# Window attention woven into a two-layer product: transposes and value products of a token tile issued one or two slots later, tiles at another spacing

## The chip, the cores and the metric

One core of a Trainium2 chip runs the whole program. The metric is the device time of one execution in microseconds (us). The kernel before takes 881.43 us, the median of three runs (880.12 to 882.33). Differences under 0.3% (2.6 us) are about what a measurement of this kernel cannot tell from none.

## The reference

All data is float32. 4 sequences of 576 tokens have 8 heads of 64 channels; a token sees itself and the 63 tokens before it. The result, as 2304 tokens of 512 channels, goes through two two-layer products.

```python
scores = scale * np.matmul(q, k.transpose(0, 1, 3, 2))
mask = (rel >= 0) & (rel < window)                  # window = 64
attn = np.exp(scores - max); attn = attn / (np.sum(attn, axis=-1, keepdims=True) + 1e-09)
x = np.matmul(attn, v)                              # -> (2304, 512)
h = x @ w_in;  g = np.maximum(0.01 * h, h);              y = g @ w_out      # 512 -> 2048 -> 512
h = y @ w_in2; g = np.maximum(h, 0) + np.log1p(np.exp(-np.abs(h))); out = g @ w_out2
```

## The kernel before

Each large product is made of three TensorE products of rounded halves (`three`, L530 to L533), because an operand is kept as a high and a low part (`xh`, `xl`, `gh`, `gl`).

The tokens are cut into 6 chunks of 384, a chunk into 3 tiles of 128 (`TPC`). For a chunk and one of 16 slices `j` of the hidden layer there is a step: `gemm1(c, j)` makes 12 products into the PSUM tile `ph` and has ScalarE and VectorE make `g`, `gh` and `gl` from it; `gemm2`, two steps behind (`SKEW`), makes 12 products into the four PSUM tiles `o`. The attention of chunks 0 and 1 is done in the head, whose order is written out by hand (`HEAD`) and which the change does not touch. The attention of chunks 2 to 5 (tiles 6 to 17) is woven into the steps of earlier chunks: a step has two slots, one ahead of `gemm1` and one ahead of `gemm2`, so an even slot's work stands before the 12 products of `gemm1` and an odd slot's before the 12 of `gemm2`. Chunk 2 is woven into a visit of 8 steps (16 slots), chunks 3, 4 and 5 each into a visit of 16 steps (32 slots). `attention_slots` says which piece of which tile goes into which slot; the slots of a tile are counted from `s`, the slot of its scores:

- `tile_a` (slot s-1): VectorE transposes of q and k (L690, L693), ScalarE's scaled copy `qbd`, and a copy on GpSimd.
- `tile_bp` (s): the scores, 32 small TensorE products into two PSUM tiles `ps` (L703). Then for each half of the heads `tile_bm` (mask, VectorE, L719), `att_bn` (maximum, VectorE) and `att_be` (four exponentials with their sums, ScalarE, L439).
- `att_bs`, `att_bx` (s and s+1): reciprocals of the sums on VectorE, and one multiplication on GpSimd for each half (L452), which gives `sm`.
- `att_cp`, `att_ca`: four TensorE transposes of `sm` for each half into PSUM tiles `pt` (L461), and their copies `at` on ScalarE (L467).
- `tile_d`: the value products `po` (32 on TensorE, L733: 16 with the rows `vs` of v, then 16 with `vn`), then `xh` on ScalarE (L743) and `xl` on VectorE (L744). The last tile's `xh` and `xl` complete the chunk, whose `gemm1` follows in the next visit.
- Loads on SyncE's queue: `load_qk(t + 1)` in slot s+1 (for even tiles the blocks of two tiles, in 32 or 64 transfers; nothing for odd ones), and `load_v(t + 1)` beside `tile_d`.

`ps`, `pt` and `po` share two PSUM buffers in this stretch (tag `att`), so a tile's scores need both, its transposes need both, and its value products need one. `sm` has three buffers in SBUF, `at` two, the rows of v three.

The kernel is written in a framework whose planner fixes each engine's order when the program is built: it goes by program order, passes over an instruction whose inputs or buffers it does not yet expect to be ready, and goes by its own estimates of time. At run time each engine works through its list in that order.

Of the kernel before, what the change touches and what calls it, by code (L numbers as in the profile page):

```python
# [20 lines left out]
def tile_window_attention_two_mlps(  # L21
# [40 lines left out]
    TPC = T // P  # L62
# [432 lines left out]
    def new_x(m, c):  # L495
        xh, xl = (x_tile(nm, f"{nm}_{m}_{c}", [P, NK, T], F32R) for nm in ("xh", "xl"))
        X[m, c] = (xh, xl)
        return xh, xl
# [247 lines left out]
    def attention_slots(c, n_slots):  # L746

        at = {n: [] for n in range(n_slots)}
        x = new_x(0, c)
        for n in range(TPC):  # L750
            t = c * TPC + n
            s = 1 + (n_slots - 8) * n // (TPC - 1)
            two = ((t, 0), (t, 1))
            at[s - 1].append((tile_a, (t,)))
            at[s].append((tile_bp, (t,)))
            at[s] += [(f, (g,)) for g in two for f in (tile_bm, att_bn)]
            at[s].append((att_be, (two[0],)))
            at[s + 1] += [(f, (two[0],)) for f in (att_bs, att_bx)]
            at[s + 1] += [(f, (two[1],)) for f in (att_be, att_bs, att_bx)]
            if t + 1 < NT // P and t + 1 != BY_DVE:  # L760
                at[s + 1].append((load_qk, (t + 1,)))
            at[s + 3] += [(f, (g,)) for f in (att_cp, att_ca) for g in two]
            at[s + 5].append((tile_d, (t, *x)))
            if t + 1 < NT // P:
                at[s + 5].append((load_v, (t + 1,)))
        return at

    def ticker(keys):
# [67 lines left out]
    for item in HEAD:  # L836
        n = len(item.rstrip("0123456789"))
# [39 lines left out]
    for n, (c, j, s, e, nxt) in enumerate(steps):  # L877
        if n < CUT + NF:
            continue
        if s:  # L880
            left = next(i for i in range(n, len(steps)) if steps[i][3]) - n + 1
            slots = attention_slots(nxt, 2 * left) if nxt is not None else {}
            slot = 0
        for u in range(2):
            for f, a in slots.get(slot, ()):
                f(*a)
            slot += 1
            if u == 0:
                gemm1(c, j)
        if c == NC - 1:  # L890
            for f, *a in prepare.get(j, ()):
                later(f, *a)
        if n >= SKEW:
            gemm2(*steps[n - SKEW][:4])
# [13 lines left out]
    for p in range(2, NF // 2):  # L908
        n = last_of[p - 2]
# [66 lines left out]
```

## Time and profile before

| | before |
|---|---|
| median of three runs | 881.43 us (880.12 to 882.33) |
| the profiled execution's own time | 884.99 us |
| its span, first to last instruction | 883.2 us |
| granted TensorE clock, mean of the span | 0.994 of full speed |
| TensorE matmul records busy | 854.2 us, 97% |
| VectorE, ScalarE, GpSimd busy | 538.1, 408.1, 49.5 us |

The profile is of one execution, which took 3.6 us more than the median of the runs. The stretch with which the change is concerned, the steps that carry attention, lies from about 152 to 440 us after the span's start. In the views, PE is TensorE, PEld its weight loads, DVE VectorE, ACT ScalarE, POOL GpSimd and SPq SyncE's queue of transfers. Matmuls overlap: a busy record covers one product from its start to its modelled end, and the next one starts before that.

### The profile page before, as it was taken

How to read it: one execution, taken by the hardware profiler on the slowest of the kernel's cores; microseconds unless marked ns; L12 is line 12 of the kernel's file. 1: busy time of each engine (PE TensorE's matmuls, PEld its weight loads, DVE VectorE, ACT ScalarE, POOL GpSimd, SP SyncE). 2: the span in 40 equal slices, each digit the busy share in tenths (PEclk: the TensorE clock that was granted, in tenths of full speed). 3: DMA queues.
4: the chain of work that ended last, by engine and by line, in shares of the span. 5: the costliest groups of instructions: out<-in, count | busy, mean ns of one | idle time of the engine just before them, and what ended most of it. 6: DMA issues, size and time to landing. Idle time of an engine off the chain costs nothing.

```text
span 883.2 us, 14592 instructions
## 1 busy us (share of the span) xinstructions
PE 854.2 (97%) x5424; PEld 799.9 (91%) x5424; DVE 538.1 (61%) x1052; ACT 408.1 (46%) x966; POOL 49.5 (6%) x66
## 2 busy tenths in 40 slices
PE   6799899999999999999999999999999999999998
PEld 5789899898999989999999999999999888888886
DVE  5798762535333233321357689777799986766664
ACT  6786652644434344442445532222244754545443
POOL 3111000211101011100000000000000000000000
PEclk9899999999999999999999999999999999999999
DMA  9767552243133420210132145544487544444432
GB/s 203 191 196 224 167 128 40 64 81 92 28 56 55 99 57 26 60 24 13 37 127 77 54 161 194 165 155 155 155 307 253 190 133 126 117 127 122 117 102 65
DMA packets 150278, 104.76 MB, mean 119 GB/s; under 512 B 104896, under 2 KB 129472, under 8 KB 150208
## 3 DMA queue, kind: packets, MB, share of 16 engines
q1 hardware_dynamic: 150208, 103.84, 41.3%
q8 instruction: 42, 0.69, 0.3%
q14 instruction: 28, 0.23, 0.1%
HBM read 75.50 MB, written 28.31 MB: 118 GB/s over the span
## 4 chain that ended last, share of the span: by engine, by line
PE 79%; DVE 6%; SPq 4%; DMA 4%; ACT 4%; issue 2%; POOL 1%; POOLq 0%; DVEq 0%; ACTq 0%
PE f L531 7%; PE f L532 7%; PE f L533 7%; PE ph L531 6%; PE ph L533 5%; PE ph L532 5%; PE o L531 5%; PE o L532 5%; PE o L533 5%; PE p_s L532 4%; PE p_s L531 4%; PE p_s L533 4%; SPq L336 3%; PE p_a L532 3%; PE p_a L531 3%; PE p_a L533 3%
## 5 line engine op out<-in xcount | busy, mean ns | idle before, releaser
L563 DVE TENSOR_TENSOR gl<-g,gh 128x384 fp32r<-128x384 f32 x96 | 58.2, 606 | 181.5 <-ACT gh L557 144.1
L531 PE MATMUL o<-gh,w 128*128 128x384 f32 x384 | 130.9, 341 | 2.4 <-ACT part L577 2.3
L531 PE MATMUL ph<-xh,w 128*128 128x384 f32 x384 | 131.4, 342 | 0.0
L532 PE MATMUL o<-gl,w 128*128 128x384 f32 x384 | 129.1, 336 | 0.3 <-DVE gl L563 0.2
L532 PE MATMUL ph<-xl,w 128*128 128x384 f32 x384 | 128.5, 335 | 0.0
L533 PE MATMUL ph<-xh,w 128*128 128x384 f32 x384 | 128.5, 335 | 0.0
L533 PE MATMUL o<-gh,w 128*128 128x384 f32 x360 | 121.0, 336 | 0.0
L551 ACT ACTIVATE g<-ph 128x384 f32<-128x384 f32 x96 | 46.9, 488 | 148.9 <-PE ph L533 148.7
L531 PE MATMUL f<-w,s 128*128 128x512 f32 x234 | 91.0, 389 | 0.0
L532 PE MATMUL f<-w,s 128*128 128x512 f32 x234 | 91.0, 389 | 0.0
L533 PE MATMUL f<-w,s 128*128 128x512 f32 x234 | 91.0, 389 | 0.0
L662 ACT ACTIVATE s<-s 128x512 f32<-128x512 f32 (+1 forms) x80 | 46.8, 588 | 72.8 <-DVE s L661 72.5
L531 PEld LDWEIGHTS o<-gh,w 128*128 128x128 f32 x384 | 72.6, 189 | 5.2 <-ACT part L577 2.5
L532 PEld LDWEIGHTS o<-gl,w 128*128 128x128 f32 x384 | 72.7, 189 | 0.8 <-DVE gl L563 0.8
L531 PEld LDWEIGHTS ph<-xh,w 128*128 128x128 f32 x384 | 72.1, 188 | 1.0
L664 DVE SCALAR_TENSOR_TENSOR s<-s,s 128x512 f32<-128x512 f32 (+1 forms) x80 | 50.7, 638 | 36.4 <-ACT s L662 36.0
L532 PEld LDWEIGHTS ph<-xl,w 128*128 128x128 f32 x384 | 72.2, 188 | 0.0
L533 PEld LDWEIGHTS ph<-xh,w 128*128 128x128 f32 x384 | 72.1, 188 | 0.0
L533 PEld LDWEIGHTS o<-gh,w 128*128 128x128 f32 x360 | 68.0, 189 | 0.0
L439 ACT ACTIVATE sm<-sm,nm 128x128 f32<-128x128 f32 x144 | 55.9, 390 | 24.5 <-DVE nm L428 24.4
L234 DVE TENSOR_TENSOR s<-s,s 128x512 fp32r<-128x512 f32 (+1 forms) x80 | 50.9, 638 | 12.8 <-ACT s L233 12.4
L233 ACT CAST s<-s 128x512 fp32r<-128x512 f32 (+1 forms) x80 | 46.0, 576 | 23.4 <-PE f L532 20.1
(169 smaller groups left out, 1645.5 us busy)
## 6 DMA issues: line engine op xcount, KB each, us to landing
wraw<-in_moe_w_out_dram SPq DMA_DIRECT2D x32, 512.0 KB, 4.7
wraw<-in_moe_w_in_dram SPq DMA_DIRECT2D x32, 512.0 KB, 4.7
s<-hd SPq DMA_DIRECT2D x64, 256.0 KB, 2.7
hd<-h_xh SPq DMA_DIRECT2D x12, 768.0 KB, 4.5
hd<-h_xl SPq DMA_DIRECT2D x12, 768.0 KB, 4.2
x2d<-x SPq DMA_DIRECT2D x24, 192.0 KB, 2.0
x_stage<-x2d SPq DMA_DIRECT2D x24, 192.0 KB, 2.5
out_dram<-s SPq DMA_DIRECT2D x18, 256.0 KB, 2.4
```

Of the source, the lines that this page charges most:

```text
L233: i = nc.scalar.copy(hi, a)
L234: j = nc.vector.tensor_tensor(lo, a, hi.bitcast(F32), ALU.subtract)
L336: nc.sync.dma_start(a[i * TB : (i + 1) * TB, p, off : off + n].rearrange("r (n c) -> r n c", c=TB), src[b, 2 * p + h, s : s + n, d : d + T ...
L439: nc.scalar.activation(sm[:, p, :], sm[:, p, :], AF.Exp, bias=nm[:, p : p + 1], accum_out=sums[:, p : p + 1],)
L531: nc.tensor.matmul(ps, wh, xh, start=start, stop=False)
L532: nc.tensor.matmul(ps, wh, xl, start=False, stop=False)
L533: nc.tensor.matmul(ps, wl, xh, start=False, stop=stop)
L551: nc.scalar.activation(g, ph, AF.Prelu, alpha=0.01)
L563: b = nc.vector.tensor_tensor(gl, g, gh.bitcast(F32), ALU.subtract)
L662: nc.scalar.activation(g, g, AF.Softplus)
L664: nc.vector.scalar_tensor_tensor(g, h, 0.0, g, ALU.max, ALU.add)
```

## The change

In the visits of 32 slots the scores of the three tiles stand in slots 1, 12 and 23 (before: 1, 13, 25), the transposes and their copies five slots after the scores (before: three), and the value products with the load of the next tile's v rows seven after (before: five). In the visit of 16 slots the scores stay in slots 1, 5 and 9, the transposes come four slots after them and the value products six. So there a tile's transposes come into the slot of the next tile's scores (slots 5 and 9), ahead of them. The last tile's value products stand in slot 30 of 32 as before, and in slot 15 of 16 (before: 14).

```diff
@@ attention_slots
+            late = n_slots > 16
-            s = 1 + (n_slots - 8) * n // (TPC - 1)
+            s = 1 + (11 if late else 4) * n
...
-            at[s + 3] += [(f, (g,)) for f in (att_cp, att_ca) for g in two]
-            at[s + 5].append((tile_d, (t, *x)))
+            at[s + 4 + late] += [(f, (g,)) for f in (att_cp, att_ca) for g in two]
+            at[s + 6 + late].append((tile_d, (t, *x)))
             if t + 1 < NT // P:
-                at[s + 5].append((load_v, (t + 1,)))
+                at[s + 6 + late].append((load_v, (t + 1,)))
```

## Rows read from the trace of the kernel before

**Rows 1.** The page's first part: busy us (share of the span) and instructions.

```profile
PE 854.2 (97%) x5424; PEld 799.9 (91%) x5424; DVE 538.1 (61%) x1052; ACT 408.1 (46%) x966; POOL 49.5 (6%) x66
```

**Rows 2.** TensorE's waits, 145 to 290 and 290 to 450: us, times, longest.

```profile
PE pt L461 <- POOL sm L452: 5.1, 7, 1.4
...
PE pt L461 <- POOL sm L452: 3.4, 6, 1.0
```

**Rows 3.** Busy us (count) in the attention steps: PE, PEld, DVE, ACT, POOL; clock.

```profile
152.00:440.00 288.00, 279.46 (x2223) 266.34 (x2223) 101.34 (x198) 122.38 (x358) 31.16 (x33) 1.00 0.24 53
```

**Rows 4.** PE in order of time, tiles 6 and 7: start us, us, what.

```profile
153.91 0.34 PE L533 MATMUL ph<-xh,w 128*128 128x384 f32 x1
154.18 1.10 PE L703 MATMUL ps<-kT,qbd 64*64 64x128 f32 x32
...
155.49 0.34 PE L532 MATMUL o<-gl,w 128*128 128x384 f32 x1
...
161.39 0.34 PE L533 MATMUL o<-gh,w_last 128*128 128x384 f32 x1
161.69 0.66 PE L461 MATMUL pt<-ident,sm 128*128 128x128 f32 x4
163.23 0.66 PE L461 MATMUL pt<-ident,sm 128*128 128x128 f32 x4 [0.88 <-POOL sm L452]
...
163.90 0.34 PE L532 MATMUL ph<-xl,w 128*128 128x384 f32 x1
...
168.95 0.34 PE L533 MATMUL o<-gh,w 128*128 128x384 f32 x1
...
169.74 0.64 PE L733 MATMUL po<-at,vn 128*64 128x64 f32 x16
...
170.59 0.34 PE L532 MATMUL ph<-xl,w 128*128 128x384 f32 x1
...
174.40 0.34 PE L533 MATMUL o<-gh,w 128*128 128x384 f32 x1
174.58 1.03 PE L461 MATMUL pt<-ident,sm 128*128 128x128 f32 x8
...
175.62 0.34 PE L532 MATMUL ph<-xl,w 128*128 128x384 f32 x1
```

**Rows 5.** PE in order of time, tile 9's transposes and tile 17's.

```profile
208.79 0.66 PE L461 MATMUL pt<-ident,sm 128*128 128x128 f32 x4 [1.44 <-POOL sm L452]
...
209.81 0.34 PE L531 MATMUL ph<-xh,w 128*128 128x384 f32 x1
210.47 0.65 PE L461 MATMUL pt<-ident,sm 128*128 128x128 f32 x4 [0.32 <-POOL sm L452]
...
419.07 1.10 PE L703 MATMUL ps<-kT,qbd 64*64 64x128 f32 x32
...
426.28 0.34 PE L533 MATMUL o<-gh,w 128*128 128x384 f32 x1
...
428.23 0.34 PE L532 MATMUL ph<-xl,w 128*128 128x384 f32 x1
```

**Rows 6.** GpSimd in order of time, tile 6's second half.

```profile
162.14 1.04 POOL L452 TENSOR_TENSOR sm<-sm,sums 128x512 f32<-128x512 f32 x1 [0.50 <-DVE sums L448]
```

**Rows 7.** ScalarE in order of time: after a `gemm1`, and tile 7's copies.

```profile
154.80 0.51 ACT L557 CAST gh<-g 128x384 fp32r<-128x384 f32 x1
...
175.21 1.08 ACT L467 COPY at<-pt 128x512 f32<-128x512 f32 x2 [1.05 <-PE pt L461]
```

**Rows 8.** SyncE's queue in order of time, loads for tiles 7 and 8.

```profile
169.95 0.39 SPq L300 DMA_DIRECT2D vn<-in_v_dram  x1
170.39 10.29 SPq L336 DMA_DIRECT2D kblocks<-in_k_dram  x19
```

**Rows 9.** The page's part on transfers: count, KB each, us to landing.

```profile
vn<-in_v_dram SPq DMA_DIRECT2D x16, 256.0 KB, 4.2
```

**Rows 10.** VectorE in order of time, tile 6's low part.

```profile
171.72 0.69 DVE L744 TENSOR_TENSOR xl<-po,xh 128x512 fp32r<-128x512 f32 x1
```

## Prediction, written before the result was known

> **What bounds the kernel now.** I read the page's busy shares first, then TensorE's waits, then TensorE's instructions in order of time around the twelve tiles, and last what the other engines and SyncE's queue do in the same places. The shares say that TensorE has work for 97% of the span and that no other engine passes 61% [rows 1]. So a change here can only win what TensorE stands still in the attention steps, and loses what it adds to that. In these steps TensorE's waits have one line: the transposes `pt` wait for GpSimd's `sm`, 5.1 + 3.4 = 8.5 us in 13 waits, none over 1.44 us [rows 2, 5]. The busy view agrees, with 288 - 279.46 = 8.5 us not busy, and the granted clock there is 1.00, so no part of the loss is a slower clock [rows 3].
>
> What this costs is better read from start to start, since a matmul record runs on to its modelled end while the next one has begun. From the second to the last of the 36 matmuls between tile 6's scores and its transposes, 34 intervals take 161.39 - 155.49 = 5.90 us, so 0.1735 us each and 2.08 us for the 12 of a half step, which is one slot [rows 4]. A piece of attention costs the distance from the last matmul before it to the second one after it, less two such intervals (0.347): scores 155.49 - 153.91 - 0.347 = 1.23 us, value products 170.59 - 168.95 - 0.347 = 1.29, and the eight transposes of tile 7, the only tile that does not wait, 175.62 - 174.40 - 0.347 = 0.87 [rows 4]. Tile 6's transposes take 163.90 - 161.39 = 2.51 where tile 7's take 1.22, a loss of 1.29 us, though its record shows a wait of 0.88; tile 17's take 428.23 - 426.28 = 1.95, a loss of 0.73 [rows 4, 5].
>
> The whole loss comes from one balance. From tile 6's scores (slot 1 of a visit of 16) to tile 17's (slot 25 of a visit of 32, two full visits between) are 15 + 64 + 25 = 104 half steps, or 104 x 2.082 = 216.6 us, and eleven tiles of 1.23 + 0.87 + 1.29 = 3.40 us, or 37.4 us. That is 254.0 us; the rows show 419.07 - 154.18 = 264.9 [rows 4, 5]. So eleven tiles lose 10.9 us, and with tile 17's 0.73 the twelve lose 11.7 us, all at their transposes, since no other wait stands in that stretch.
>
> The Trainium skill (Perfetto Trace Analysis, Identifying the Most-Contended Engine) holds that matmul busy time is a poor measure of distance from the limit because matmuls are pipelined. The trace agrees: busy time puts the loss at 8.5 us and distances between starts at 11.7; with the smaller loss the sum below would end at 874.9 in place of 871.7.
>
> **The change, part by part.** It removes, adds and resizes no instruction; it moves them.
>
> *Transposes later.* What is late today is the end of a chain: mask and maximum on VectorE, eight exponentials on ScalarE, reciprocals on VectorE, two multiplications on GpSimd. Tile 6's second multiplication ends at 162.14 + 1.04 = 163.18 and its transposes start at 163.23 [rows 4, 6]. One slot more is 2.08 us and two are 4.16. The nine tiles in visits of 32 lose at most about 2.1 us each even where two waits add up (1.44 + 0.32 recorded for tile 9) [rows 5], so two slots cover them. Tile 6 loses 1.29, and tile 8's and all other recorded waits are shorter than the longest of 1.44 [rows 2], so one slot covers those as well. Gain: 11.7 us. It hides in matmuls of `gemm1` and `gemm2` that TensorE has to do anyway. Lower bound of this part: were the chain itself to stretch, none of it.
>
> *Transposes ahead of the next scores (slots 5 and 9 of the 16).* The scores need both PSUM buffers that the transposes have just filled, so they wait for ScalarE's two copies. Tile 7's two copies end at 175.21 + 1.08 = 176.29, 1.71 us after its transposes started [rows 4, 7]. In an odd slot `g` and `gh` of the `gemm1` just done may stand ahead on ScalarE: `gh` ended at 155.31, 1.13 us after the point where the next work of TensorE started (154.18) [rows 4, 7]; two copies then end 1.13 + 1.08 = 2.21 after it. The scores would otherwise start 0.87 after it. So a stall of 0.84 to 1.34 us, twice: 1.7 to 2.7 us. Below that bound: the planner has in the kernel before put `gemm1` matmuls between two halves of transposes (209.81, between those at 208.79 and 210.47) [rows 5]; where it fills this gap with `gemm2` in the same way, the cost is 0. I take 1.0 us for both, nearer the filled case because that row shows the filling left 0.32 us.
>
> *Value products and their loads later.* `tile_d` keeps its distance of two slots from the transposes, so its wait for ScalarE's copies is no tighter. `load_v` goes with it. In the visits of 32 it comes two slots later and is needed eleven slots after that (22.9 us) against 4.2 us to landing [rows 9]: nothing. In the visit of 16 one order flips: `load_v(7)` was listed in slot 6 ahead of `load_qk(8)`; now it is in slot 7, behind it. The load at 169.95 in the middle of the k blocks of tile 8 is by my count of loads the `vn` rows of tile 7; 19 block transfers follow it, until 170.39 + 10.29 = 180.68 [rows 8]. Were they all first, it would be issued at about 180.3 and land at 184.5. Tile 7's value products then stand in slot 11: 154.18 plus ten half steps (20.8), three scores (3.7), two transposes (1.7) and one set of value products (1.3) is 181.7, and their `vn` half begins 169.74 - 168.95 - 0.17 = 0.6 us later, at 182.4 [rows 4]. So a wait of 0 (if the load keeps its place) to 2.1 us; behind it TensorE's whole list waits. I take the middle, 1.0.
>
> *Visit's end.* Tile 8's value products come one half step before `gemm1` of its chunk instead of two. Tile 6's `xl` ended at 171.72 + 0.69 = 172.41, 3.46 us after the last matmul before the value products; the first matmul that would read it comes 0.347 + 1.29 + 2.08 = 3.72 after it [rows 4, 10]. Covered by 0.3 us, so nothing; were one such VectorE operation of 0.69 to stand ahead of it, 0.4 us.
>
> *Spacing of 11 slots for 12.* Every slot is followed by the same 12 matmuls and no `att` buffers collide (last use at s+7, next at s+11): nothing.
>
> Sum: -11.7 + 1.0 + 1.0 + 0 = -9.7 us. Against the profiled execution's own 884.99 us that is 875.3; it ran 3.6 us above the median, and I carry the difference over unscaled: 881.43 - 9.7 = 871.7 us. Bounds: all costs nothing, 881.43 - 11.7 = 869.7; all costs full (2.7 + 2.1 + 0.4 = 5.2), 874.9.
>
> **The rivals.**
>
> 1. *The chain stretches into the room.* VectorE's and ScalarE's lists are planned anew, and transposes of q or adds of `x` may be put ahead of a mask. For it: tile 9 waits longer than tile 6 (1.44 and 0.32 against 0.88) [rows 4, 5], so the chain is not the same everywhere. Against: the six waits after 290 us add up to only 3.4 us [rows 2], so most tiles are alike. If half the loss returns, 881.43 - 5.85 + 2.0 = 877.6 us.
> 2. *The wait only changes its name.* The value products wait for `at`, or the scores for buffers, as long as the transposes did. For it: two `att` buffers. Against: distances two slots and more everywhere but in slots 5 and 9. Time: 881.4 us.
> 3. *The change does not do what it says.* The planner, not the slot, orders the engines, so transposes might be put where they were. Against: today they stand exactly 36 matmuls behind the scores, three slots [rows 4]. Time: 881.4 us.
> 4. *Slower: v rows late.* `vn` of tile 7 loses its place on SyncE's queue. If it fell also behind the next pair's 32 block transfers, at 10.29 / 19 = 0.54 us each 17.3 us, it would be issued near 197.6 and land near 201.8 [rows 8, 9]; TensorE would wait 19.4 us at 182.4, and the sum would be -11.7 + 1.0 + 19.4 = +8.7, 890.1 us. It decides from the landing on at which the wait exceeds 10.7 us, 193.1. Against: these blocks are listed in a later visit.
>
> **How the numbers follow.** Forecast (between its bounds, 869.7 to 874.9): 0.76. Rival 1: 0.10; rival 2: 0.06; rival 3: 0.04; rival 4: 0.04. Under 0.3% (2.6 us) a measurement of this kernel can hardly tell a difference from none. Faster by more: forecast and rival 1, 0.86. Within: rivals 2 and 3, 0.10. Slower: rival 4, 0.04. The range goes from 869.4 (the lower bound, less 0.3 for rounding of the intervals) to 877.6, the time of rival 1, and leaves out the rest of the cases.
>
> **What would show it.** After: no wait of `pt` for `sm` in the attention steps, or under 1 us in all; eight transposes in one row at every tile of the visits of 32; from tile 6's scores to the end of tile 17's transposes about 10 us less on TensorE, apart from the changed slots. In slots 5 and 9 the scores right behind the transposes with a wait for ScalarE's `at` near 1 us, or `gemm2` matmuls between. A wait of `po` for a load of v at tile 7 if the queue's order flipped. The prediction is wrong if `pt` still waits, which means that the chain is not what I timed; if `po` or `ps` wait in its place; or if the waits are gone and the time is not.

## The result, and the profile after

The changed kernel takes 870.51 us (median of five runs, 869.23 to 872.04) against 881.43 us (880.12 to 882.67) beside it: a ratio of 0.9875, 95% interval 0.9856 to 0.9894, so 10.9 us less. In a later comparison the same two kernels gave 870.70 and 881.05 us, 0.9883 (0.9861 to 0.9904). Forecast were 871.7 us (869.4 to 877.6) and a gain.

The page's first part, to be read beside [rows 1]: TensorE's share rises from 97 to 98%, and the other engines do the same work.

```profile
PE 849.8 (98%) x5424; PEld 799.4 (92%) x5424; DVE 537.4 (62%) x1052; ACT 406.2 (47%) x966; POOL 48.7 (6%) x66
```

TensorE's waits from 145 to 450 us (line waited for: us, times, longest), where [rows 2] had 8.5 us in 13 waits of `pt`: one wait of 0.2 us is left, at the scores of tile 7.

```profile
PE ps L703 <- ACT at L467: 0.2, 1, 0.2
```

The stretch of [rows 3] (busy us and count of PE, PEld, DVE, ACT, POOL; clock): TensorE is busy in 287.80 of 288 us, where it was in 279.46, at the same granted clock.

```profile
152.00:440.00 288.00, 287.80 (x2257) 278.67 (x2256) 108.27 (x215) 127.58 (x371) 29.77 (x32) 1.00 0.26 59
```

TensorE in order of time (start us, us, what) at the places of [rows 4] and [rows 5]: tiles 6 and 7, then the scores of tile 8, the transposes of tile 9 and the scores of tile 17.

```profile
149.84 1.10 PE L703 MATMUL ps<-kT,qbd 64*64 64x128 f32 x32
...
159.13 0.34 PE L533 MATMUL ph<-xh,w 128*128 128x384 f32 x1
159.31 1.04 PE L461 MATMUL pt<-ident,sm 128*128 128x128 f32 x8
160.10 0.42 PE L531 MATMUL o<-gh,w 128*128 128x384 f32 x1
160.36 0.34 PE L532 MATMUL o<-gl,w 128*128 128x384 f32 x1
160.53 0.33 PE L533 MATMUL o<-gh,w 128*128 128x384 f32 x1
161.03 1.99 PE L703 MATMUL ps<-kT,qbd 64*64 64x128 f32 x32 [0.17 <-ACT at L467]
162.95 0.44 PE L531 MATMUL o<-gh,w 128*128 128x384 f32 x1
163.23 0.33 PE L532 MATMUL o<-gl,w 128*128 128x384 f32 x1
...
172.17 1.03 PE L461 MATMUL pt<-ident,sm 128*128 128x128 f32 x8
...
173.57 0.34 PE L531 MATMUL o<-gh,w 128*128 128x384 f32 x1
173.94 1.58 PE L703 MATMUL ps<-kT,qbd 64*64 64x128 f32 x32
...
175.73 0.34 PE L533 MATMUL o<-gh,w 128*128 128x384 f32 x1
...
179.64 0.58 PE L733 MATMUL po<-at,vn 128*64 128x64 f32 x14
...
206.60 1.04 PE L461 MATMUL pt<-ident,sm 128*128 128x128 f32 x8
...
401.19 1.10 PE L703 MATMUL ps<-kT,qbd 64*64 64x128 f32 x32
```

Every tile's eight transposes are now one row. Tile 6's take 160.36 - 159.13 = 1.23 us where they took 2.51, which is what tile 7's took before (1.22). The balance of the prediction, made again: from tile 6's scores to tile 17's are now 15 + 64 + 23 = 102 half steps, 212.4 us, and eleven tiles, 37.4 us, together 249.8; the rows show 401.19 - 149.84 = 251.35. The loss is 1.55 us where it was 10.9, and tile 17's 0.73 is gone too: 10.1 us less of loss inside the stretch, and the runs show 10.4 and 10.9 less.

The new cost is where it was looked for. In slots 5 and 9 of the visit of 16 the scores stand behind the previous tile's transposes with three or four `gemm2` matmuls between, and their 32 products are stretched to 1.99 and 1.58 us (1.10 before). From the last matmul before them to the second after, tile 7's take 163.23 - 160.53 - 0.347 = 2.35 and tile 8's 175.73 - 173.57 - 0.347 = 1.81, against 1.23: 1.12 + 0.58 = 1.7 us.

SyncE's queue at the place of [rows 8] (start us, us, what, count): all 30 block transfers for k of tile 8 that were left now go ahead of the `vn` rows of tile 7.

```profile
160.32 15.42 SPq L336 DMA_DIRECT2D kblocks<-in_k_dram  x30
175.84 0.39 SPq L300 DMA_DIRECT2D vn<-in_v_dram  x1
```

One warning on the spans of the two profiled executions: 868.7 against 883.2 us is a difference of 14.5 us, more than the runs show. Tile 6's scores start at 149.84 us in one and at 154.18 in the other, and among the profiles below at anything from 147.6 to 155.5, with no relation to what was changed (155.5 in the kernel of the visits of 32 alone, whose median is 871.71 us and whose profiled execution took 876.58). The head, which is not changed, differs between these profiles: in that of the kernel before, the granted clock is 0.50 (1.2 GHz) from 29.4 to 36.1 us and from 94.2 to 97.5 us, in that of the changed kernel only from 30.1 to 33.4 us. So the comparisons below are made inside the stretch.

### The profile page after: what moved, and what is told of

Read it like the earlier page. It is cut to its first block, busy times and chain, and to the rows that moved or that the text cites. A ratio compares the mean times of both kernels' runs of the same rounds, so it can differ in the third digit from the quotient of the medians.

```text
span 868.7 us, 14599 instructions
## 1 busy us (share of the span) xinstructions
PE 849.8 (98%) x5424; PEld 799.4 (92%) x5424; DVE 537.4 (62%) x1052; ACT 406.2 (47%) x966; POOL 48.7 (6%) x66
## 4 chain that ended last, share of the span: by engine, by line
PE 90%; DVE 3%; DMA 3%; ACT 1%; issue 1%; SPq 1%; POOL 0%; ACTq 0%; DVEq 0%
PE f L533 8%; PE f L532 8%; PE f L531 8%; PE o L531 7%; PE ph L531 7%; PE o L532 7%; PE o L533 7%; PE ph L533 7%; PE ph L532 7%; PE p_s L533 4%; PE p_s L531 4%; PE p_s L532 4%; PE p_a L533 3%; PE p_a L531 3%; PE p_a L532 3%; DMA wraw<-in_moe_w_out_dram 2%
```

## The experiments

For each kernel the balance above was made from its own profile: the time from tile 6's scores to tile 17's, less 2.0824 us (12 x 5.90 / 34) for each half step and 3.40 us for each of eleven tiles. What is left is what TensorE lost there, to about 0.1 us. It leaves tile 17's transposes out.

| kernel | from, to (us) | half steps | loss (us) | waits of `pt` (us, times) | median us, beside before | ratio (95%) |
|---|---|---|---|---|---|---|
| before | 154.18, 419.07 | 104 | 10.9 | 8.5, 13 | 881.43 | |
| changed | 149.84, 401.19 | 102 | 1.6 | none | 870.51, 881.43 | 0.9875 (0.9856 to 0.9894) |
| spacing alone | 151.49, 412.25 | 102 | 11.0 | 8.8, 13 | 882.37, 881.46 | 1.0009 (0.9991 to 1.0027) |
| visits of 32 alone | 155.47, 407.25 | 102 | 2.0 | 1.5, 2 | 871.71, 881.46 | 0.9870 (0.9843 to 0.9898) |
| visit of 16 alone | 149.67, 414.17 | 104 | 10.5 | 7.0, 11 | 882.25, 881.46 | 1.0008 (0.9994 to 1.0022) |
| one slot | 151.21, 404.14 | 102 | 3.1 | 2.1, 3 | 873.22, 881.46 | 0.9905 (0.9878 to 0.9931) |
| no multiplication | 148.88, 403.39 | 104 | 0.5 | none | 869.01, 882.40 | 0.9860 (0.9826 to 0.9894) |
| twice, before | 151.23, 446.21 | 104 | 41.0 | 27.0, 22 | 911.49, 882.40 | 1.0334 (1.0300 to 1.0369) |
| twice, changed | 149.33, 401.91 | 102 | 2.8 | 0.9, 1 | 872.65, 882.40 | 0.9898 (0.9857 to 0.9939) |
| transposes alone | 148.63, 404.36 | 102 | 5.9 | 1.5, 2 | 877.22, 882.40 | 0.9937 (0.9915 to 0.9958) |
| changed, again | 150.00, 401.38 | 102 | 1.6 | none | 870.70, 881.05 | 0.9883 (0.9861 to 0.9904) |
| no shared slot | 147.62, 399.33 | 103 | -0.2 | none | 869.90, 881.05 | 0.9866 (0.9846 to 0.9886) |

**Spacing alone.**

```diff
-            s = 1 + (n_slots - 8) * n // (TPC - 1)
+            s = 1 + (11 if n_slots > 16 else 4) * n
```

> The tiles stand in slots 1, 12 and 23 of the visits of 32, and nothing else is changed. Chain theory (TensorE stands still at the transposes because the softmax chain ends later than three slots after the scores): the waits stay, 11.7 us in all, and the time stays at 881 us within 2.6. Rival, the new plan (the spacing, and with it another order of loads and of VectorE's and ScalarE's lists, made the gain): clearly under 881, towards 871.

Measured 882.37 us, 1.0009 of before, with the waits and the loss of before. The spacing is worth nothing by itself.

**Visits of 32 alone.**

```diff
-            s = 1 + (n_slots - 8) * n // (TPC - 1)
+            late = 2 * (n_slots > 16)
+            s = 1 + (11 if late else 4) * n
...
-            at[s + 3] += [(f, (g,)) for f in (att_cp, att_ca) for g in two]
-            at[s + 5].append((tile_d, (t, *x)))
+            at[s + 3 + late] += [(f, (g,)) for f in (att_cp, att_ca) for g in two]
+            at[s + 5 + late].append((tile_d, (t, *x)))
```

(`load_v` goes with `tile_d`, here and below, and its lines are left out.)

> The changed positions in the visits of 32 slots alone; in the visit of 16 all stays as before. Chain theory: nine of twelve tiles stop waiting, 11.7 - 1.29 - 0.83 = 9.6 us less, 871.8 us; the three tiles of the visit of 16 still lose 2.1 us. Rival, the new plan: the load order of tile 7's v rows is not changed here, so if that made the gain, about 881.

Measured 871.71 us. The loss falls by 8.9 us, and by tile 17's 0.73 beyond the balance, 9.6 in all; the two waits left are those of tiles 6 and 8, 1.5 us as recorded. So nearly all of the gain comes from these visits, and none of it needs the new order of tile 7's rows of v.

**Visit of 16 alone.**

```diff
+            late = n_slots <= 16
-            at[s + 3] += [(f, (g,)) for f in (att_cp, att_ca) for g in two]
-            at[s + 5].append((tile_d, (t, *x)))
+            at[s + 3 + late] += [(f, (g,)) for f in (att_cp, att_ca) for g in two]
+            at[s + 5 + late].append((tile_d, (t, *x)))
```

> The changed positions in the visit of 16 slots alone. Chain theory: 2.1 us of waits go and the scores in slots 5 and 9, one after the other's transposes, cost 1.7 us as in the changed kernel, net 0.4 us less, 881.0 us, not to be told from before. Rival, the new plan: most of the 10.9 us, 871.

Measured 882.25 us, not to be told from before. The balance shows why: the loss falls by 0.4 us only, since the loss at tiles 6 and 8 that goes (2.1 us from start to start) is paid for with the stretched scores (1.7 us).

**One slot.** The kernel of the visits of 32 alone, with `late = n_slots > 16`: the added distance is one slot in place of two.

> In the visits of 32 slots the transposes come four slots after the scores and the value products six (one slot later instead of two), spacing 11; the visit of 16 as before. Chain theory: no tile lost more than 2.1 us and a slot is 2.08 us, so the waits go here as well: 871.8 us, the same as with two slots; at most 0.5 us is left at tiles 9 and 13. Rival, the chain stretches into the room it is given: about half the waits come back, 876.6 us.

Measured 873.22 us; the interval holds the 871.8 of the chain theory and not the 876.6 of its rival. The loss is 3.1 us, of which the visit of 16 has 2.1. A single wait came back, at tile 9 (0.60 us recorded). By the balance tiles 9 and 13 lose about 1 us, where at most 0.5 was expected for the two; at tile 13 no wait is recorded, but its eight transposes take 1.36 us instead of 1.04. TensorE, the two halves of tile 9, then tile 13 (start us, us, what):

```profile
206.32 0.60 PE L461 MATMUL pt<-ident,sm 128*128 128x128 f32 x4
207.53 0.66 PE L461 MATMUL pt<-ident,sm 128*128 128x128 f32 x4 [0.60 <-POOL sm L452]
...
310.21 1.36 PE L461 MATMUL pt<-ident,sm 128*128 128x128 f32 x8
```

**No multiplication.** This shortens the chain and moves nothing; tiles 6 to 17 are the ones named by a tuple.

```diff
 def att_bx(gb):
-        nc.gpsimd.tensor_tensor(
-            sm, sm, sums.unsqueeze(2).to_broadcast([P, NP, P]), ALU.mult
-        )
+        if not isinstance(gb, tuple):
+            nc.gpsimd.tensor_tensor(
+                sm, sm, sums.unsqueeze(2).to_broadcast([P, NP, P]), ALU.mult
+            )
```

> The kernel before, all slots as they were, with GpSimd's two multiplications of a tile by the reciprocal sums left out for tiles 6 to 17: these rows of the attention stay unnormalised. Chain theory: the chain ends 1.2 to 1.3 us sooner, which is more than the 0.7 us that an ordinary tile loses; left are about 0.8 us at tile 9 and 0.4 at tile 13, so about 10.5 us less, 871 us. Rival, the two PSUM buffers or the distance of the slots in itself made the loss: 881 us.

Measured 869.01 us with every slot where it was before, and no wait of TensorE is recorded in the stretch. Of the 1.2 us that had been expected to stay at tiles 9 and 13, tile 9 shows 0.6: its eight transposes take 1.66 us where the others take 1.04, and that is all that the balance has left. Tile 9's transposes, then the busy time in the stretch:

```profile
199.77 1.66 PE L462 MATMUL pt<-ident,sm 128*128 128x128 f32 x8
...
145.00:435.00 290.00, 289.88 (x2299) 280.09 (x2298) 103.15 (x212) 128.25 (x372) 5.79 (x9) 1.00 0.26 58
```

So the end of the chain is the cause, and the slots matter only as far as they put the transposes behind it: taking a multiplication of 1.04 us and its start off the chain and adding one or two slots of 2.08 us give the same. That excludes the PSUM buffers and the distance in itself.

**Twice, in both kernels.**

```diff
 def att_bx(gb):
-        nc.gpsimd.tensor_tensor(
-            sm, sm, sums.unsqueeze(2).to_broadcast([P, NP, P]), ALU.mult
-        )
+        for _ in range(2 if isinstance(gb, tuple) else 1):
+            nc.gpsimd.tensor_tensor(
+                sm, sm, sums.unsqueeze(2).to_broadcast([P, NP, P]), ALU.mult
+            )
```

> The kernel before with GpSimd's multiplication by the reciprocal sums done twice for tiles 6 to 17, so these rows of the attention are scaled wrongly. Chain theory: the second half of each tile is ready about 1.6 us later (its own multiplication starts when the first half's two are done), and since nothing covers it TensorE loses up to 12 x 1.6 = 19 us more, 900 us; less where the planner sees the longer chain and puts gemm matmuls ahead. Rival, the chain is not what TensorE waits for: 881 us.

> The changed kernel with the same doubling. Chain theory: the room that the slots give takes it up but for tiles 6, 9 and 13, whose transposes stood 0.46, 0.93 and 1.44 us behind the end of the chain: 1.1 + 0.7 + 0.1 us, so about 872.5 us. Rival, the change works by another way than by cover: as much slower as the kernel before becomes by the doubling, about 889 us.

Before: 911.49 us, 29.1 more. After: 872.65 us, 2.0 or so more than the changed kernel. The same 24 added multiplications cost 29 us in one kernel and about 2 in the other (1.2 by the balance), which is what cover means. In the changed one, one wait is recorded in the stretch, at the second half of tile 6 (0.88 us); tiles 9 and 13, where 0.8 us was expected, have transposes of 1.37 and 1.19 us in place of 1.04, about 0.5 us together.

In the kernel before they cost 10 us more than the 19 that were expected at most, for two reasons. The chain ends later than was expected: at tile 11, 8.43 us after the scores without the doubling (267.43 + 1.04 - 260.04) and 10.43 with it (277.14 + 4.59 - 271.30), 2.0 us more and not 1.6, or 24 us over twelve tiles; the recorded waits are 27.0 us to the end of the stretch at 460 us, the longest 2.2. GpSimd at tile 11, without and with the doubling:

```profile
267.43 1.04 POOL L452 TENSOR_TENSOR sm<-sm,sums 128x512 f32<-128x512 f32 x1 [0.52 <-DVE sums L448]
...
277.14 4.59 POOL L453 TENSOR_TENSOR sm<-sm,sums 128x512 f32<-128x512 f32 x4 [3.84 <-DVE sums L448]
```

And the granted clock falls. TensorE in order of time at tile 6, the kernel before with the doubling (start us, us, what):

```profile
159.88 0.66 PE L462 MATMUL pt<-ident,sm 128*128 128x128 f32 x4 [1.10 <-POOL sm L453]
160.29 0.42 PE L532 MATMUL ph<-xh,w 128*128 128x384 f32 x1
162.19 1.11 PE L462 MATMUL pt<-ident,sm 128*128 128x128 f32 x4 [1.47 <-POOL sm L453]
...
163.42 0.52 PE L534 MATMUL ph<-xh,w 128*128 128x384 f32 x1
163.74 0.52 PE L532 MATMUL ph<-xh,w 128*128 128x384 f32 x1
```

And the same kernel's stretches of time after it (busy us and count of PE, PEld, DVE, ACT, POOL; then the granted clock):

```profile
162.10:166.70 4.60, 4.51 (x15) 4.13 (x15) 0.41 (x1) 0.59 (x1) 0.03 (x1) 0.50 0.28 68
...
168.60:176.00 7.40, 7.40 (x68) 7.08 (x69) 5.08 (x11) 5.24 (x20) 2.68 (x3) 1.00 0.25 52
```

Around the second wait the clock goes to 0.50, the level of 1.2 GHz, and stays there for more than 5 us, and matmuls start 0.32 us apart in place of 0.1735. From 150 to 460 us the mean is 0.96:

```profile
150.00:460.00 310.00, 282.95 (x2141) 267.65 (x2140) 101.60 (x195) 120.88 (x353) 58.89 (x57) 0.96 0.22 47
```

A mean of 0.96 over 310 us is worth some 25 us at half speed, in which, at these two distances between starts, about 25 x (1 - 0.1735 / 0.32) = 11 us are lost. This is an estimate, and may be too high, since TensorE waits in part of that time; how the 10 us that the sum had missed divide between the later chain and the clock is not shown.

**Transposes alone.** The kernel of the visits of 32 alone with `tile_d` and `load_v` left at `s + 5`, the slot into which the transposes now come.

> In the visits of 32 slots the transposes come five slots after the scores, and the value products stay there too, in the same slot behind them, instead of two slots later; spacing 11; the visit of 16 as before. Chain theory: the waits for the softmax go (9.6 us), but the value products now need copies that ScalarE has not made; by the price that the scores paid in slots 5 and 9 of the changed kernel, 0.6 to 1.1 us a tile for nine tiles, 871.8 + 5 to 10, so 877 to 881 us. Rival, where the value products stand is of no matter because the planner fills in gemm matmuls: 871.8 us.

Measured 877.22 us: about half of the gain of the visits of 32 is given back. The loss is 5.9 us against 2.0 with the value products moved too, 3.9 more over the eight tiles 9 to 16, so 0.5 a tile, just below the price taken from slots 5 and 9. TensorE at tile 11 (start us, us, what): the value products are put between matmuls of `gemm1`, two of them first, then the rest.

```profile
259.41 1.04 PE L461 MATMUL pt<-ident,sm 128*128 128x128 f32 x8
...
260.73 0.33 PE L733 MATMUL po<-at,vs 128*64 128x64 f32 x2
260.99 0.45 PE L533 MATMUL ph<-xh,w 128*128 128x384 f32 x1
261.27 0.34 PE L531 MATMUL ph<-xh,w 128*128 128x384 f32 x1
261.54 0.62 PE L733 MATMUL po<-at,vs 128*64 128x64 f32 x13
```

No wait is recorded there, and yet each such place costs half a microsecond, where the value products now stand in two pieces: the planner did not hide it wholly. So `tile_d` had to move along.

**No shared slot.** The changed kernel, and beside it on the same chip one in which the visit of 16 has scores in slots 0, 5 and 9.

```diff
-            s = 1 + (11 if late else 4) * n
-            at[s - 1].append((tile_a, (t,)))
-            at[s + 4 + late] += [(f, (g,)) for f in (att_cp, att_ca) for g in two]
-            at[s + 6 + late].append((tile_d, (t, *x)))
+            s = 1 + 11 * n if late else (0, 5, 9)[n]
+            at[max(s - 1, 0)].append((tile_a, (t,)))
+            at[s + 5 if late else (4, 8, 13)[n]] += [(f, (g,)) for f in (att_cp, att_ca) for g in two]
+            at[s + 7 if late else (6, 10, 15)[n]].append((tile_d, (t, *x)))
```

> The changed kernel once more, beside the next one on the same chip: 870.5 us, 0.9875 of before.

> The changed kernel with the visit of 16 slots laid out so that no tile's transposes share a slot with another's scores: scores in slots 0, 5 and 9, transposes in 4, 8 and 13, value products in 6, 10 and 15. Chain theory: no wait of transposes, and the 1.7 us that the scores in slots 5 and 9 cost are gone: 1.7 us less than the changed kernel beside it, about 868.8, at the edge of what can be measured; in the trace the scores of tiles 7 and 8 stand in one row of 1.10 us. Rival, the stall in those slots was of no matter: no difference, and the same balance of starts.

Measured 870.70 and 869.90 us. The trace is clear, the timing is not: the loss of the stretch goes from 1.6 to nothing (-0.2, the rounding of the balance), the scores of tiles 7 and 8 are one row of 1.10 us again, but 0.8 us between medians with overlapping intervals cannot be told from none.

```profile
160.14 1.10 PE L703 MATMUL ps<-kT,qbd 64*64 64x128 f32 x32
...
171.86 1.10 PE L703 MATMUL ps<-kT,qbd 64*64 64x128 f32 x32
```

## Why the prediction was right

**What bounds the kernel.** TensorE's standing still at the transposes was all there was to win, and the balance of starts measured it: 11.7 us before, 1.6 after. The kernel without the multiplication shows it from the other side. The Trainium skill (Perfetto Trace Analysis, Identifying the Most-Contended Engine) warns against matmul busy time, since matmuls are pipelined; the trace agrees: over the stretch of 288 us the busy time rose by 8.3 us, while distances between starts give a gain of 10.1 us and the runs 10.4 and 10.9.

**Transposes later (-11.7).** Right. In the visits of 32 all nine tiles stopped waiting. Tile 9 loses the most before the change, from start to start 2.2 us (from the last matmul before its transposes to the second after them 211.14 - 207.01 = 4.13, less six intervals and the undisturbed 0.87; the prediction had 2.1 at most), and there the chain ends 0.93 us ahead of its transposes. In the visit of 16 one slot sufficed for tile 6 by 0.46 us: its second multiplication ends at 157.81 + 1.04 = 158.85 and the transposes start at 159.31. GpSimd in order of time:

```profile
157.81 1.04 POOL L452 TENSOR_TENSOR sm<-sm,sums 128x512 f32<-128x512 f32 x1 [0.50 <-DVE sums L448]
```

**Transposes ahead of the next scores (+1.0).** The mechanism was right, the size low: 1.7 us, within the bounds of 0 to 2.7. The planner did fill the gap with `gemm2` matmuls, but let the scores begin while one of their two buffers was not free yet, and so stretched them. ScalarE at tile 6's copies shows it: the scores of tile 7 start at 161.03, as the first copy ends (160.98), and the second copy, behind the `gh` that the prediction had named, ends at 161.88, in the middle of their 1.99 us.

```profile
160.40 0.58 ACT L467 COPY at<-pt 128x512 f32<-128x512 f32 x1
160.87 0.52 ACT L557 CAST gh<-g 128x384 fp32r<-128x384 f32 x1
161.28 0.60 ACT L467 COPY at<-pt 128x512 f32<-128x512 f32 x1
```

**Value products and loads later (+1.0).** The order flipped as worked out: the load stands behind all block transfers, 175.84 - 149.84 = 26.0 us after tile 6's scores, where 180.3 - 154.18 = 26.1 had been worked out. The wait was 0, but not for the reason that the prediction gave for its lower bound, that the load keeps its place. The load landed 3.3 us after its issue, not 4.2, so at 179.1, and the first product that needs it started at 179.64 with no wait recorded, 29.8 us after tile 6's scores. The prediction had that product 28.2 us after them (182.4 - 154.18); the 1.7 us by which the stretched scores put it off were not in that figure. Half a microsecond was to spare. So one term was 0.7 too low and the other 1.0 too high, and the first helped to make the second nothing.

**Visit's end and spacing (0).** Right: no wait of `gemm1` at the visit's end, and the spacing alone measured 1.0009.

**The sum.** -11.7 + 1.7 + 0 + 0 = -10.0, where -9.7 was forecast; the runs show -10.9 and -10.4. What is between is less than these runs resolve. That -9.7 came so close is in part luck: the two costs were each mis-sized, and their errors cancel.

**The rivals.** The chain did not stretch into the room. Counted from the start of a tile's scores, its last multiplication ends at the same time before and after the change: 8.43 and 8.45 us at tile 11 (before as above, after 255.04 + 1.04 - 247.63), 10.61 and 10.61 at tile 9. The scores of tile 9 and its last multiplication, before (the first two rows) and after:

```profile
199.80 1.10 PE L703 MATMUL ps<-kT,qbd 64*64 64x128 f32 x32
209.14 1.27 POOL L452 TENSOR_TENSOR sm<-sm,sums 128x512 f32<-128x512 f32 x1 [0.41 <-DVE sums L448]
...
195.06 1.10 PE L703 MATMUL ps<-kT,qbd 64*64 64x128 f32 x32
204.40 1.27 POOL L452 TENSOR_TENSOR sm<-sm,sums 128x512 f32<-128x512 f32 x1 [0.41 <-DVE sums L448]
```

The loss did not move to the value products in the changed kernel, though it can, as the kernel with the transposes alone shows, where they took half the gain back. The planner kept to the slots. The loads of v came late on the queue, but behind 30 transfers, not behind the next pair's.

## What to carry to other kernels

Where one engine is the bound and works through its list in order, measure its losses from start to start against the pace of an undisturbed stretch; recorded waits showed 8.5 of 11.7 us here. A chain on other engines need not be made shorter (though that worked here too, in the kernel without the multiplication); enough work of the bound engine ahead of its consumer does the same: compare the chain's end with the consumer's place, add the slots that cover it, and move along what consumes the consumer, or half the gain comes back. Before adding distance look at what then shares a slot and its buffers, since in the short visit that took back nearly all of it.

## What had not been expected of the hardware

In the kernel before with the doubled multiplication, waits of 1.10 and 1.47 us at tile 6, with one matmul and four transposes between them, came with a granted clock of 0.50 (1.2 GHz) for more than 5 us, with matmuls 0.32 us apart in place of 0.1735; with the single wait of 0.88 us that tile 6 had before, and the 1.44 and 0.32 of tile 9, the stretch showed 1.00. No wait there is longer than 2.2 us. But the waits alone do not settle it: tiles 11 and 14 of that kernel have the same two waits, of 0.50 and 1.77 us, and the clock stays at 1.00 behind those of tile 11 and falls to 0.50 behind those of tile 14. What tells the two apart is not shown. TensorE and the stretches (busy us and count of PE, PEld, DVE, ACT, POOL; then the granted clock), tile 11 first:

```profile
279.36 0.66 PE L462 MATMUL pt<-ident,sm 128*128 128x128 f32 x4 [0.50 <-POOL sm L453]
281.79 0.66 PE L462 MATMUL pt<-ident,sm 128*128 128x128 f32 x4 [1.77 <-POOL sm L453]
276.00:290.00 14.00, 11.72 (x95) 10.85 (x94) 3.26 (x9) 5.78 (x19) 4.44 (x4) 1.00 0.21 43
...
366.31 0.66 PE L462 MATMUL pt<-ident,sm 128*128 128x128 f32 x4 [0.51 <-POOL sm L453]
368.74 0.66 PE L462 MATMUL pt<-ident,sm 128*128 128x128 f32 x4 [1.77 <-POOL sm L453]
369.70:373.00 3.30, 3.30 (x12) 3.30 (x11) 0.00 (x0) 0.32 (x1) 0.00 (x0) 0.50 0.02 5
```

So doubling a multiplication of 1.04 us on GpSimd cost 29 us over twelve tiles, about a fifth more than the 24 us by which the chain ended later. The Trainium skill (TensorE: Matmul & The Clock Gate, Part 1) says that the clock gate sets TensorE's rate by how busy the engine has lately been, with 1.2 GHz as the lower level; the trace agrees with the level, at which matmuls start 0.32 us apart.
